# Ten half-tiles take their threshold on GpSimd: one exponential in place of an exponential and a masked pass

## The chip, the cores and the metric

One NeuronCore of a Trainium2 chip runs the whole program. It has five engines that run their own instruction streams in order: TensorE (PE in the profile, with its weight loads apart as PEld), VectorE (DVE), ScalarE (ACT), GpSimd (POOL) and SyncE (SP), which here issues most of the DMA transfers. The metric is the device time of one execution in microseconds (us); lower is better.

## The reference

Sixty-four heads (8 batches of 8 heads, 576 positions, head width 64) of attention with a threshold, and then a three-way maxout feed-forward layer over 4608 tokens:

```
scores = scale * q @ k.T                       # scale = 1/8
thresh = max(scores, axis=-1) - tau            # tau = 0.02
scores = where(scores >= thresh, scores, -1e9)
attn   = exp(scores - max(scores)); attn /= sum(attn) + 1e-9
x      = attn @ v                              # heads side by side: 4608 x 512
h      = max(x @ w1, x @ w2, x @ w3)           # 512 -> 768
out    = h @ w_out                             # 768 -> 512
```

Every row of scores keeps only the entries within tau of its maximum; all others count as zero.

## The kernel before, in words

**Tiles.** The heads are taken four at a time (a quad, two per batch). A quad has 9 chunks of 128 partitions by two halves of 576 keys; the unit of work is such a half-tile, 128 x 576, and there are 288 of them, called tiles below. For each tile the program does: `S`, the scores in fp32 on TensorE into one of four PSUM slots (`sc`); `m`, the row maximum on VectorE (`nm` receives it); then one of two ways to the numerators, chosen tile by tile by a digit of the table `MASKED`:

- digit 0: ScalarE takes a Prelu of the scores that multiplies the positive side (the excluded entries) by one and the kept side by 2^-100 (`e`, tile `z<-sc,nm`), and then an exponential with scale -2^100, which brings the kept side back and sends the excluded side to zero, with the row sum as a second result (`n`). Two passes on ScalarE, and one on VectorE, the maximum.
- digit 1: the maximum pass also writes the negated scores to SBUF (`z<-sc`); ScalarE takes the exponential (`e`, `z<-z,nm`); VectorE then keeps what is at least exp(-tau) and sums it (`k`, a SCALAR_TENSOR_TENSOR). One pass on ScalarE and two on VectorE.

**After the numerators.** For the first batch (the first 36 tiles, quads 0 and 1) the numerators go straight into the bf16 tile `P`, unnormalised; the sums are gathered in `sums`, inverted for a whole part (`R`), spread over a PSUM tile by small matmuls (`D`, tile `d`), copied to `wide` (`b`), and multiplied in when the attention product is copied to `xt` (`w`). For all other batches the numerators go to fp32 `z`, and GpSimd scales them into `P` (`p`, `P<-z,rs`). Then SyncE issues a DMA transpose of `P` (`t`, `ptq<-P`), TensorE multiplies by v (`O` and `N`, tile `o`), the result becomes `xt`, and TensorE runs the feed-forward matmuls (`F` and `B`, tiles `ph` and `po`). There are six `P` buffers, each for a pair of tiles, and a new one waits until the transpose of the one six before it has read it. There are eight `z` tiles.

**Other work of GpSimd.** It copies halves of the transposed queries to the other partitions (`q`, `qs<-qt`; scores need them), and casts v (`y`) and the weights (`z` in the table) to bf16.

**What sets the order.** `ORDER` is a string written out by hand or by a planner; each letter issues one step, so it fixes the order of the instructions on every engine and of the DMAs in SyncE's queue. `_Ordered` chains the instructions of each engine in that order, and an instruction that waits holds up all behind it on its engine. Nearly all instructions go through that helper, so the profile names them by line 92 and by their tiles.

Of the kernel before, what the change touches and what calls it, by code (L numbers as in the profile page):

```python
# [40 lines left out]
ORDER = """
mS2S3lmS1meenemelllgkllT0S2aqmlmeS3lmgT1lllT0eqckT2ancS0mtqS1qmennktyS3eteS2mznmS1eeS0mnlS3eS2S1mmS3netmegke
S2mS0mmyeS3znnRytyltleeS1nmkkeS0mmeeS2mS1enS0T3kmmktgltlemS1D2aS0eT3blekmmteS2D0O1ckmlO3bNwRwS0mneeD1knS3beT
2nD1tllabS0mS2ketnO1lRktmetmO3qNqtwqwzenT2nS0S1zncS3qymmS2mmeeS1S3D0S2mkmtD1elbeemneS0kmbkT3S1kegmatS2qS3neT
0memknneS2O1O3cNtS0remkwtqerT2pnaRmpS1D0gekrS2bmtlwneS0S3D1mmpplleblppzO2eO1mrqpNnekpS0wwS2nnmzF3S1S0emrmrmk
glBepqpF1pF2ethgzBevT3nBF0S1nncBvhS3S2pmrmgF0ekeT1BatnmrF3vS1BS0peF2rmpypS1lpBnvmezF3nhzBS2mpenekqvS1F0F3mtm
BqerkrBpgvepptT2cS1T0hnamttS3mnrS2tF0myBeS1ppeS2yvnplF3rS0nmemteeBlF1meqptS2pvT3BcmnF0tlS3znkphgglBemS1rvmS2
O3npemO0rknrNeewpF1xpS2qpS0ltntmF3lmneeBBS2S0rvhmF1tntpzleS3mBpF0S2empztvenrpBmpvS1mnS3S2enF0emrpS3pktS1pnme
rmmepBekuS2mkunenrS1S3pF0T2pmmtaBeueukpS1rpqeklmeS2tO3mprO0ekNS1lltlwlS2xmF3nF0BmepT1kBehrcF2nT3T1BvcppS0tlq
aqnllvF3qlmS1mrBprF2S0nekheBnmpvtF3S1BF2eS0mvtprmBypnpS1ehpytpS3mtoS2oeelmtmS0F3lF1meBkevryBT2yenF0vapT3cBT2  # L50
S1lS3naqhpF2qS0rkmBpmmrF3npeS1vempteneBvF2S0ktpmltrllBF3S1lnhnmBqrvpneelS0S2mpmO1ekreO3NT0xS2wcmS3mnpqpnF1F0
pBekpBvS2ertlS3F1htmtltmS0pBnemepynrF3eS2vS0mmrT1atppqeBS2pnpF1vF3meultkS0klT1enormkT2BaS2peS0ortcmnmuurS1pe
T2qpF3cS2mpenenpS0kmetrBmltS1S2puymlueeqpS0pylomO3mO1knNerekxwS0pmS2F3S1npnqmBF2elS0kmtBerkheF3pS1nmeypvBtrm
noF2leS0vpBS3rrmnpmpphS1ppF0etmS2emllBeF1nF3BtevkrpS0BvS2nS1hmmtleS3lmmetF2tkF0eBpleT1BvrvanT3nF2cS1BnmF0S3B
rhkF2mpeT1vnrBpprveaS0S3nmT1S2pqpncmpS0meeeqmeS1tO3pqmtotlloeO2ltqNF0S1klwBxrpkppS3mrhmF2S0epBmF3nenS1pvBF0m
F2nleBBtottvkS3hF0keF1rurvpmT2BeapkppyrpvS1S3mnS2S0pnemF1mtS2emkS3rpBenepltS0memkmrutpuS3neS2emF1rmpqkynpS3p
qeBemS0uuS3O2kmemekO1NeS0rwT3xoF1olppnT2mnT0BcS3aS2rncqhF0qtF1pBtemmpBkevrF3eS2vlmpnBptnlS0S1S2hermmempS3F0y
pmF1BBelrteoevnF2T3F0akkqvBBS3nhkymF1pqpnF2verBBS0rvtpmhnS3S1F2mrmlpBpeS0evlmS3eF1pnS2BmnleF3mtllvrlttS0eppp
tyBmS1ehF2lepT3BmltnS0lnltcS1rkvO3O2tmNpmeprT1nnexrapkwS0pqF2qyemT1T3cpBF0S1anepkBS3hvF2S0mreBF1mekmrnvF3qBe
S2vS0unpS3tS1omlrmeppqptlmmnF2pktT0BpecS1eekryuT3uaS0mnS2lomtmrtleF3enpS1kpS2qppnemmS0BmkerppeueqS1S0mnurO2k  # L60
mO1NkwxT0S3eeS1cmpmF2F0kkeBBhF3eF2pvrBS1nnBvpttS0hmemS3mrppF1rpS2BeenmeF0S3vBF1nkvmS2mlnBS0otolhF3llterlmF1k
BlpypvpBtvteeprS2F0rT3BpS1nnrmpmaS3mtpheS0S2emnF3eT1T0amecBS2ttoS0evyymmS1ppeO3mpqneO2NenqxF0kktF1wBT3lolrlk
lBpS2vphS0cmnF1mtlteS3nqrtBmrpF0vrpqpF2lekBeBpnhF1S3vmT0tlpBS2lS3avmpF0tF1mBrnelekS2evutppmrS3qppS1nS0nmF2mr
mS1peekenpS3BemmeS0rkS1emuS3tlT0ueT2mcknrannpepF1S0mS2qppBmtotlmlttkrrpeueS0qqmS2lO3ueemoeO0opptpkklNwS1lS2x
F3mS0BnemehF1kT2mrcnpBS0F3rvS2BltlpnmF1nepmeveS0pkmBS3httnF2eF1mBrBekF0nS3vrBprvpypppS2nmhemeS1S0F2pF3mmBeBr
T1eS0kvnapS2vF1nS3mnBrmmreS2F0pheS1meeBqpnS3mvmeypS1tpS2etlO0qO3mNpmT2neytF1xtlkkrtnweS3ppT0cramBF2S0Bnehvpp
meS1rF3qqmT2BF0ncveT2ktnBF3vS1mrnarBhppS0lF2T3qppeBmcS0S1ovmF3mneT2naepBvS0S2enF3mkmrkqpqueenF1nS3tmS0T2cpqB
eupurrS2mmottoS3pS0mttneelotpmS1O2mkkO0rNwrpeexpneF3nkpS0S2S1mBemS0euuppmF1erkS2tltlBptmrF3S0lhtpmeyppBeS1mv
O0O2NenmxpS3S1kF0mxemrS2kBF1enF3vBermF0tBhpyppyektBvS1pmF2F3vBkS1BF0nmehS2vrBmtpO3eotpnevO1NkF0S2krmnrpxpxBh
F3S1eBF0mS2F1BnvpmBrS3vS2S0ehemmF1kppmnF3rBvkBF2F0BF1ehBtkvevoF2pptkttO3O0NuprBwS2xS0vmmpeS3ekF1S2pmF0oeBmrB  # L70
okettF3peuokoruoF2uhF1pkkF3hvvruF2pF1F3hppF0pvvF2F1vvF3F0F2hvtovhtF1F3F0F2htvF1voF3O0uvO2NvF1xwF3hF2F0vF3vhF
2F0F3hvF2vvF0F3F2vF0hF3hovF2vF0F3vhF2vvF0vBuuF3BuouoF2uooo
"""


# [731 lines left out]
```

## Time and profile before

| | |
|---|---|
| median of 3 runs | 441.56 us (440.37 to 443.75) |
| the profiled execution | 439.98 us, of which 438.2 us from first to last instruction (the span) |
| busy: PE, DVE, ACT, POOL | 96%, 91%, 88%, 66% of the span |
| mean granted TensorE clock | 1.00 |

A row of the profile's groups reads: line, engine, operation, output tile <- input tiles, shapes, count | busy time, mean ns of one | idle time of the engine just before these instructions and what ended it. On DVE and ACT the recorded durations of neighbours overlap a little; what an instruction costs its engine is read from start to start in the timeline.

### The profile page before, as it was taken

Reading aid. Unit: us, or ns where it says so; the run is one execution under the profiler, and the core shown is the slowest. Engines: PE = TensorE matmul, PEld = TensorE weight load, DVE = VectorE, ACT = ScalarE, POOL = GpSimd, SP = SyncE. Lnnn points to the kernel's source line nnn. Section 1 sums busy time; section 2 is a strip of 40 time slices with the busy share of each in tenths; the row PEclk is TensorE's granted clock in tenths of the full one; section 3 lists DMA queues with packets and bytes.
Section 4 is the critical chain, followed back from the end, with each engine's and each line's share of the span. In section 5 each row is a group of like instructions: output and inputs, shape, how many; then the busy total and the mean of one; then the engine's idle time right before and its main releaser. Section 6 shows DMA issues by size and latency. Waiting matters only on the chain.

```text
span 438.2 us, 14262 instructions
## 1 busy us (share of the span) xinstructions
PE 420.6 (96%) x5313; PEld 306.9 (70%) x5313; DVE 398.2 (91%) x1105; ACT 387.0 (88%) x784; POOL 288.5 (66%) x370
## 2 busy tenths in 40 slices
PE   7679889999999999999999999999999999999995
PEld 5446458776787767867787767877677776777762
DVE  3999999989999999999999999999999999999641
ACT  5999999999999999988999999989999999875422
POOL 3704288978688697596867885678759677554500
PEclk9999999999999999999999999999999999999999
DMA  7999999999999999999899998979989997485602
GB/s 252 302 241 206 221 229 261 237 244 193 211 192 225 229 200 193 205 174 256 185 203 216 222 190 206 212 201 219 201 220 186 246 150 154 110 160 128 177 14 109
DMA packets 212773, 87.45 MB, mean 200 GB/s; under 512 B 185824, under 2 KB 199648, under 8 KB 212704
## 3 DMA queue, kind: packets, MB, share of 16 engines
q1 hardware_dynamic: 212000, 85.69, 92.4%
q8 instruction: 42, 0.69, 0.7%
q10 hardware_dynamic: 704, 0.85, 0.6%
q14 instruction: 27, 0.22, 0.2%
HBM read 34.60 MB, written 9.44 MB: 101 GB/s over the span
## 4 chain that ended last, share of the span: by engine, by line
PE 81%; ACT 9%; DMA 3%; issue 2%; DVE 2%; POOL 2%; SPq 0%; POOLq 0%; DVEq 0%
PE ph L92 30%; PE sc L92 27%; PE po L92 11%; PE o L92 9%; ACT z L92 5%; PE tp L92 3%; DMA ptq<-P 3%; ACT P L92 2%; POOL P L92 1%; DVE z L92 1%; PE warm L92 1%; DVE unused L92 1%; ACT qt L92 1%; DMA out_dram<-ob 1%; PE d L92 0%
## 5 line engine op out<-in xcount | busy, mean ns | idle before, releaser
L92 POOL TENSOR_SCALAR P<-z,rs 128x576 bf16<-128x576 f32 x252 | 206.8, 833 | 78.9 <-DVE rs L92 27.4
L92 PE MATMUL sc<-kt,qt 64*128 64x256 f32 (+2 forms) x640 | 177.1, 421 | 2.7 <-DVE z L92 1.3
L92 PE MATMUL sc<-kt,qs 64*128 64x320 f32 (+2 forms) x640 | 175.5, 410 | 4.0 <-ACT z L92 1.6
L92 PE MATMUL ph<-xt,w 64*128 64x288 bf16 (+4 forms) x2160 | 170.5, 283 | 0.4 <-ACT z L92 0.2
L92 PEld LDWEIGHTS <-w 64*128 64x128 bf16 (+1 forms) x2160 | 124.4, 94 | 33.6 <-issue 6.3
L92 DVE TENSOR_SCALAR_CACHE_REDUCE unused<-sc 128x576 bf16<-128x576 f32 x170 | 124.8, 749 | 4.0 <-PE sc L92 3.2
L92 ACT ACTIVATE z<-sc,nm 128x576 f32<-128x576 f32 x170 | 122.7, 740 | 3.4 <-DVE unused L92 1.6
L92 PEld LDWEIGHTS sc<-kt,qs 64*128 64x128 f32 (+1 forms) x640 | 91.0, 175 | 19.7 <-ACT z L92 6.3
L92 ACT ACTIVATE z<-z 128x576 f32<-128x576 f32 x151 | 102.3, 682 | 0.2
L92 PEld LDWEIGHTS sc<-kt,qt 64*128 64x128 f32 (+1 forms) x640 | 90.4, 175 | 16.3 <-DVE z L92 4.3
L92 ACT ACTIVATE z<-z,nm 128x576 f32<-128x576 f32 x118 | 89.5, 773 | 4.8 <-DVE z L92 4.6
L92 DVE TENSOR_SCALAR_CACHE_REDUCE z<-sc 128x576 f32<-128x576 f32 x118 | 87.5, 751 | 5.6 <-PE sc L92 3.1
L92 DVE SCALAR_TENSOR_TENSOR z<-z 128x576 f32<-128x576 f32 x101 | 80.1, 802 | 0.1
L92 POOL COPY qs<-qt 64x640 f32<-64x640 f32 (+3 forms) x68 | 47.8, 702 | 42.3 <-ACT qt L92 27.7
L92 PE MATMUL po<-wo,hT 64*128 64x512 bf16 (+1 forms) x480 | 53.6, 357 | 0.1
L92 ACT ACTIVATE hm<-ph 128x576 bf16<-128x576 f32 (+4 forms) x54 | 32.1, 594 | 19.9 <-PE ph L92 19.5
L92 DVE TENSOR_TENSOR hm<-ph,hm 128x576 bf16<-128x576 f32 (+4 forms) x54 | 36.9, 684 | 8.5 <-PE ph L92 8.4
L92 PEld LDWEIGHTS <-hT 64*128 64x128 bf16 (+1 forms) x480 | 26.3, 97 | 20.0 <-issue 3.9
L92 DVE TENSOR_TENSOR hT<-ph,hm 128x576 bf16<-128x576 f32 (+4 forms) x54 | 37.1, 688 | 2.4 <-PE ph L92 0.5
L92 PE MATMUL o<-ptq,vb 128*64 128x64 bf16 (+2 forms) x576 | 36.5, 275 | 0.8 <-DMA ptq<-P 0.8
L92 PEld LDWEIGHTS <-vb 128*64 128x64 bf16 x576 | 23.3, 111 | 15.7 <-issue 5.1
L92 ACT ACTIVATION_READ_ACCUMULATOR z<-z 128x1 f32 x151 | 30.0, 199 | 0.0
(40 smaller groups left out, 297.3 us busy)
## 6 DMA issues: line engine op xcount, KB each, us to landing
vm<-in_v_dram SPq DMA_DIRECT2D x32, 256.0 KB, 4.7
out_dram<-ob SPq DMA_DIRECT2D x31, 256.0 KB, 3.2
qm<-in_q_dram SPq DMA_DIRECT2D x15, 512.0 KB, 4.8
km<-in_k_dram SPq DMA_DIRECT2D x15, 512.0 KB, 5.5
stage<-in_moe_w_dram SPq DMA_DIRECT2D x9, 512.0 KB, 5.8
ptq<-P SPq DMA_TRANSPOSE x144, 4.2
stage<-in_moe_w_out_dram SPq DMA_DIRECT2D x3, 512.0 KB, 5.5
qm<-in_q_dram SPq DMA_DIRECT2D x16, 64.0 KB, 3.2
```

The lines of the kernel that those rows point to most:

```text
L92: ins = fn(*a, **kw)
```

## The change

A third kind of tile, digit 2, is added. Its maximum pass is that of digit 1 (it writes the negated scores `z`). Then GpSimd does three instructions (`d`): it adds tau to the negated maximum (`limit`, one column), compares `z` with `limit` and writes 2^100 where the entry is excluded and 0 where not into the tile's own half of `P`, and adds that to `z` in place. ScalarE then takes one exponential from `z` into `P` with the row sum (`j`): the excluded entries come out as zero. So a tile of digit 2 costs one pass on VectorE, one on ScalarE and three instructions on GpSimd.

Ten of the first 36 tiles in the table get digit 2 (tiles 5, 8, 11, 14, 17, 20, 23, 26, 29, 32). Within those 36, seven fewer have digit 1 and three fewer digit 0. Nine digits further on (up to tile 120) change between 0 and 1. In all there are now 166 of digit 0, 112 of digit 1 and 10 of digit 2, where there were 170 and 118. `ORDER` is new over its first 1086 steps (130 of 288 scores); what follows is the same, but for PSUM slots 2 and 3, which have changed names.

```
-001011001000011010101101101000010111100001101000010100001010000100001000
+001002002002102012012102112002012110100001101000010100001010000001001010
...
+    def excluded(c, r):
+        zn, far, limit = c["z", r], half_of(c, r), small.tile([128, 1], F32, name="limit", bufs=2)
+        pool.tensor_scalar(out=limit, in0=c["bias", r], scalar1=tau, scalar2=None, op0=OP.add)
+        pool.tensor_scalar(out=far, in0=zn, scalar1=limit, scalar2=1.0 / FLAT, op0=OP.is_gt, op1=OP.mult)
+        pool.tensor_tensor(out=zn, in0=zn, in1=far, op=OP.add)
+
+    def kept(c, r):
+        scalar.activation(out=half_of(c, r), in_=c["z", r], func=AF.Exp, bias=c["bias", r], scale=-1.0,
+                          accum_out=sum_of(c, r))
...
 -        if masked(c["g"], c["idx"], r):
+        if kind_of(c["g"], c["idx"], r) != "0":
...
+        elif what == "d":
+            c, r = line["d"].pop(0)
+            excluded(c, r)
+            line["j"].append((c, r))
+        elif what == "j":
+            c, r = line["j"].pop(0)
+            kept(c, r)
```

**GpSimd, second quad (the swaps of its queries, and the first casts).** Before, the stretch holds only swaps (`qs<-qt`) and casts:

```order
L92 COPY qs_262<-qt_261 64x2x320 [waits Activation_49]
L92 COPY qs_262<-qt_261 64x2x256 [waits Activation_49]
L92 CAST vb_348<-vm_129 128x1024 [waits DMAHW7_49,DMAHW6_49,Pool_49]
L92 CAST w0_63<-stage_239 128x4x256 [waits DMAHW6_49]
L92 CAST vrb_432<-vr_130 128x128 [waits DMAHW1_49,DMAHW0_49]
```

The same stretch now (`limit`, then `P<-z,limit`, then `z<-z,P` are the three instructions of one tile):

```order
L92 COPY qs_255<-qt_254 64x2x320 [waits Activation_49]
L92 TENSOR_SCALAR limit_327<-nm_297 128x1 [waits DVE_49,Pool_49]
L92 TENSOR_SCALAR P_309<-z_298,limit_327 128x576 [waits Pool_49]
L92 TENSOR_TENSOR z_298<-z_298,P_309 128x576 [waits Pool_49]
L92 COPY qs_255<-qt_254 64x2x256 [waits Activation_49,Pool_49]
L92 CAST vb_353<-vm_129 128x1024 [waits DMAHW7_49,DMAHW6_49,Pool_49]
L92 CAST w0_63<-stage_320 128x4x256 [waits DMAHW3_49]
L92 TENSOR_SCALAR limit_387<-nm_338 128x1 [waits DVE_49]
L92 TENSOR_SCALAR P_386<-z_339,limit_387 128x576 [waits Pool_49]
L92 TENSOR_TENSOR z_339<-z_339,P_386 128x576 [waits Pool_49]
```

The first three-instruction group stands between the two pairs of swaps, and each of its instructions waits for the one before it.

**GpSimd, third quad.** Here the groups stand around the swaps of the next quad's queries; some of the `P<-z,limit` also wait for a DMA (`DMAHW`), the transpose that frees the `P` buffer:

```order
L92 CAST w2_65<-stage_448 128x4x256 [waits DMAHW4_49]
L92 CAST vb_579<-vm_227 128x1024
L92 COPY qs_572<-qt_571 64x2x320 [waits PE_49,Activation_49,Pool_49]
L92 CAST vrb_647<-vr_228 128x128 [waits DMAHW0_49,Pool_49]
L92 TENSOR_SCALAR limit_651<-nm_604 128x1 [waits DVE_49]
L92 TENSOR_SCALAR P_650<-z_605,limit_651 128x576 [waits DMAHW3_49,Pool_49]
L92 TENSOR_TENSOR z_605<-z_605,P_650 128x576 [waits Activation_49,Pool_49]
L92 COPY qs_572<-qt_571 64x2x320 [waits Pool_49]
L92 TENSOR_SCALAR limit_717<-nm_687 128x1 [waits DVE_49,Pool_49]
L92 TENSOR_SCALAR P_716<-z_688,limit_717 128x576 [waits DMAHW6_49,Pool_49]
L92 TENSOR_TENSOR z_688<-z_688,P_716 128x576 [waits Pool_49]
L92 COPY qs_572<-qt_571 64x2x256 [waits Activation_49,Pool_49]
```

Before, no group stood there: the four swaps of that quad followed each other with two casts between them.

**ScalarE, tiles 8 to 14 and around.** Before, all that ScalarE waits for here comes from VectorE, from itself or from a DMA:

```order
L92 ACTIVATE z_387<-sc_368,nm_378 128x576 [waits DVE_49]
L92 ACTIVATE P_404,sums1_71<-z_373 128x576 [waits Activation_49]
L92 ACTIVATE z_406<-sc_375,nm_395 128x576 [waits DVE_49]
L92 ACTIVATE z_399<-z_399,nm_398 128x576 [waits DVE_49]
L92 ACTIVATE z_410<-z_410,nm_409 128x576 [waits DVE_49]
L92 ACTIVATE z_434<-sc_392,nm_420 128x576 [waits DVE_49]
L92 ACTIVATE P_404,sums1_71<-z_387 128x576 [waits Activation_49]
L92 ACTIVATE P_441,sums1_71<-z_406 128x576 [waits DMAHW7_49,Activation_49]
```

Now three exponentials of the new kind (`P<-z,nm`) stand in the same stretch, and each waits for GpSimd:

```order
L92 ACTIVATE P_386,sums1_71<-z_339,nm_338 128x576 [waits Pool_49]
L92 ACTIVATE z_378<-z_378,nm_377 128x576 [waits DVE_49]
L92 ACTIVATE P_401,sums1_71<-z_395 128x576 [waits Activation_49]
L92 ACTIVATE z_423<-sc_380,nm_415 128x576 [waits DVE_49]
L92 ACTIVATE z_434<-sc_408,nm_428 128x576 [waits DVE_49]
L92 ACTIVATE z_432<-z_432,nm_431 128x576 [waits DVE_49]
L92 ACTIVATE P_401,sums1_71<-z_375,nm_374 128x576 [waits Pool_49]
L92 ACTIVATE wide0_104<-d_441 128x256 [waits PE_49]
L92 ACTIVATE P_436,sums1_71<-z_419,nm_418 128x576 [waits DMAHW6_49,Pool_49]
```

ScalarE's stream has one instruction for such a tile where it had one or two, and a wait for a third engine.

More of the change, by code (lines that the diff above doesn't have):

```diff
@@ L47 @@
[L47 to L56, printed above, removed]
@@ new lines @@
+S3etznBmhT2F0BF1mrckvegprS2peBF3nmS0pBnvS1ephmF2ekmrT3BapvS0egS3F2tS1mtnF0BmrmzeBpzpnF1lehnenyBS3vkvmrS2F0eF
+1tBmBS3keqhrgtT2pT1vS0ppntaqppcS2znmmeemF1rBvenS3mnF0S2eS1rmBttF2meppevnT3BphctS0tnS1meF3mkgeS2Bqtnnpqrlvrml
+eppS1mtrkO0O3NgF1xlS2pnwS3llF0pBBmmeepkvS2ezF3mrhneS1ylmS0mprlBvnF2tS1pemBppzyS3penenvS0rmS1pF2mS0enpmekkemt
+S3rtnButS1mtrppS0F3lupkmerekT2tamkBpeS2lpquS0uS1tlO3lmenmmkO2eeetNlxS0rS1wmlF3mpneF2BT0kpypehrcnBF1T3aptlT0q
+nBlpnvcS2vF3qmS0ermrqBF1S2hekBmF3pnepvlnypS0BF1mS2vrBmyppeS3S0phememS2S1F0moeF3eBmBkT2eF1vT0rnaBnT2hpvckS3ma
@@ new lines @@
+S0F1pqneS2tqnmrprtBmF0S3vBemrF1veppS2BnS0tehF3ktplmS1lmrytlpoBmnnS2vO0relqmeO3pNeetT1S2pqppkwplotxclmS3lmnF0
+nkF1BeBS2evS3rmhmpttnlrF0S1tBS3mvpmeenerpF2S1pT0BpmlvpS3yaneF0uomeklkF2rS0T1enkT3tmacrBneS3uS1mS0tT3mupqtemt
+clF2epS1tepS3rypllltnpnpnS0kmBemtreS3mS0lqlO1pummpuO2NS0eeekS3xknrnpwmF2S1pmBqkletF3ehS0mrokqemnpBpvF2S1BrF3
+epyonmS0verrBS2mnpmpphS1ppF0etmS3emllBeF1nF2BtevkrpS0BvS3nS1hmmtleS2lmmetF3tkF0eBpleT1BvrvanT2nF3cS1BnmF0S2B
+rhkF3mpeT1vnrBpprveaS0S2nmT1S3pqpncmpS0meeeqmeS1tO2pqmtotlloeO3ltqNF0S1klwBxrpkppS2mrhmF3S0epBmF2nenS1pvBF0m
@@ new lines @@
+F3nleBBtottvkS2hF0keF1rurvpmT3BeapkppyrpvS1S2mnS3S0pnemF1mtS3emkS2rpBenepltS0memkmrutpuS2neS3emF1rmpqkynpS2p
+qeBemS0uuS2O3kmemekO1NeS0rwT2xoF1olppnT3mnT0BcS2aS3rncqhF0qtF1pBtemmpBkevrF2eS3vlmpnBptnlS0S1S3hermmempS2F0y
+pmF1BBelrteoevnF3T2F0akkqvBBS2nhkymF1pqpnF3verBBS0rvtpmhnS2S1F3mrmlpBpeS0evlmS2eF1pnS3BmnleF2mtllvrlttS0eppp
+tyBmS1ehF3lepT2BmltnS0lnltcS1rkvO2O3tmNpmeprT1nnexrapkwS0pqF3qyemT1T2cpBF0S1anepkBS2hvF3S0mreBF1mekmrnvF2qBe
+S3vS0unpS2tS1omlrmeppqptlmmnF3pktT0BpecS1eekryuT2uaS0mnS3lomtmrtleF2enpS1kpS3qppnemmS0BmkerppeueqS1S0mnurO3k
@@ L73 @@
+okettF2peuokoruoF3uhF1pkkF2hvvruF3pF1F2hppF0pvvF3F1vvF2F0F3hvtovhtF1F2F0F3htvF1voF2O0uvO3NvF1xwF2hF3F0vF2vhF
+3F0F2hvF3vvF0F2F3vF0hF2hovF3vF0F2vhF3vvF0vBuuF2BuouoF3uooo
 """
@@ L311, in masked, with kind_of @@
     def masked(g, idx, r):
-        return by_mask[2 * number[g, idx] + r] == "1"
+        return kind_of(g, idx, r) == "1"
+    def kind_of(g, idx, r):
+        return by_mask[2 * number[g, idx] + r]
     def z_of(c, r):
@@ L337, in exponents, with half_of, sum_of @@
             scalar.activation(out=zn, in_=c[r], func=AF.Prelu, bias=c["bias", r], scale=-1.0, alpha=FLAT)
+    def half_of(c, r):
+        if "P" not in c:
+            c["P"] = pp.tile([128, W], BF16, name="P")
+        return c["P"][:, r * S:(r + 1) * S]
+    def sum_of(c, r):
+        at = 2 * PLACE[c["idx"]] + r
+        return sums[c["g"]][:, at:at + 1]
+    def excluded(c, r):
[6 more added lines that the diff above has]
+                          accum_out=sum_of(c, r))
     def numerators(c, r):
@@ L342, in numerators @@
         if g < 2:
-            if "P" not in c:
-                c["P"] = pp.tile([128, W], BF16, name="P")
-            to, acc = c["P"][:, r * S:(r + 1) * S], sums[g][:, 2 * PLACE[idx] + r:2 * PLACE[idx] + r + 1]
+            to, acc = half_of(c, r), sum_of(c, r)
         else:
@@ L631 @@
                 O=products(), F=pieces())
-    line = {k: [] for k in "menkrptahvuxwcqNb"}
+    line = {k: [] for k in "menkrptahvuxwcqNbdj"}
     line["R"] = [(g, part) for part in range(2) for g in range(2)]
@@ L677, in issue @@
             c["bias", r] = maximum(c, r)
-            line["e"].append((c, r))
+            line["d" if kind_of(c["g"], c["idx"], r) == "2" else "e"].append((c, r))
+        elif what == "d":
[5 more added lines that the diff above has]
+            kept(c, r)
+            c["halves"] = c.get("halves", 0) + 1
         elif what == "e":
```

38 lines of the change are left out of this document (15 added, 23 removed).

## The prediction

> **What bounds the kernel now.** I read the page first, then busy time by stage, then the chain of waits, and last the timelines of the engines that the chain names.
>
> ```profile
> span 438.2 us, 14262 instructions
> PE 420.6 (96%) x5313; PEld 306.9 (70%) x5313; DVE 398.2 (91%) x1105; ACT 387.0 (88%) x784; POOL 288.5 (66%) x370
> POOL 3704288978688697596867885678759677554500
> ```
>
> TensorE is busy for 96% of the span, but these are averages: GpSimd's row of 40 slices starts with a hole (the digits 0, 4 and 2 in slices of 11 us), and that is where the new work goes. The stages show what bounds each (columns: length, then busy time of PE, PEld, DVE, ACT and POOL with counts, clock, DMA share, GB/s):
>
> ```profile
> 0.00:10.00 10.00, 7.92 (x71) 6.14 (x73) 2.88 (x7) 4.54 (x10) 3.21 (x12) 1.00 0.77 239
> 10.00:36.00 26.00, 19.54 (x193) 12.26 (x189) 25.86 (x75) 25.72 (x53) 10.65 (x15) 1.00 1.08 261
> 36.00:52.00 16.00, 13.97 (x155) 8.82 (x154) 15.51 (x46) 15.57 (x35) 4.76 (x5) 1.00 1.13 236
> 52.00:66.00 14.00, 11.99 (x171) 7.43 (x171) 12.97 (x39) 13.59 (x30) 11.06 (x13) 1.00 1.07 215
> 66.00:80.00 14.00, 13.91 (x200) 11.29 (x197) 13.63 (x40) 13.46 (x28) 12.70 (x16) 1.00 1.09 248
> 80.00:200.00 120.00, 119.66 (x1562) 89.39 (x1560) 115.45 (x322) 116.70 (x237) 93.48 (x120) 1.00 1.06 211
> 200.00:400.00 200.00, 199.92 (x2661) 148.41 (x2658) 192.44 (x537) 183.71 (x370) 145.46 (x186) 1.00 0.93 194
> ```
>
> From 10 to 52 us VectorE and ScalarE are both full (41.4 and 41.3 of 42 us), TensorE has holes (8.5 us), and the DMA engines are full as well. From 66 us on TensorE is full: 334 us with half a us idle. So anything gained on VectorE or ScalarE after 66 us is hidden by TensorE, and a gain must come from TensorE starting its saturated stretch earlier, or with more of its work done. It starts with the first feed-forward matmul (`ph`), and this is what stands ahead of it:
>
> ```profile
> 63.20 1.31 PE L92 MATMUL o<-ptq,vb 128*64 128x256 bf16 x31 [0.77 <-DMA ptq<-P]
> ...
> 65.89 0.60 PE L92 MATMUL ph<-xt,w 64*128 64x256 bf16 x7
> ```
>
> The chain of waits between 10 and 66 us says the same, by line and in its longest pieces:
>
> ```profile
> by line: ACT z L92 29.8%; DMA ptq<-P 21.6%; ACT P L92 17.8%; issue 10.5%; DVE z L92 4.5%; ACT qt L92 2.9%; PE o L92 2.9%; PE sc L92 2.5%; PE d L92 2.4%; DVE unused L92 1.7%; ACT wide L92 1.7%; DVE P L92 1.1%; DVE xt L92 0.8%; PE tp L92 0.6%
> 43.98 6.91 DMA ptq<-P
> 57.98 5.17 DMA ptq<-P
> ```
>
> Half of it is ScalarE (z, P, qt, wide: 52%), a fifth the transposes of `P`, and VectorE comes to 8%. The engine that the change relieves most is the one the chain names least.
>
> **The change part by part: VectorE and ScalarE.** Costs go from start to start:
>
> ```profile
> 17.05 0.73 ACT L92 ACTIVATE z<-sc,nm 128x576 f32<-128x576 f32 x1
> 17.68 0.77 ACT L92 ACTIVATE z<-z,nm 128x576 f32<-128x576 f32 x1
> 18.34 0.68 ACT L92 ACTIVATE P<-z 128x576 bf16<-128x576 f32 x1
> 18.91 0.20 ACT L92 ACTIVATION_READ_ACCUMULATOR P<-z 128x1 f32 x1
> 19.01 1.36 ACT L92 ACTIVATE z<-sc,nm 128x576 f32<-128x576 f32 x2
> ...
> L92 ACT ACTIVATE qt<-tp 128x640 f32<-128x640 f32 x3 | 2.1, 707 | 0.0
> L92 ACT ACTIVATE wide<-d 128x256 f32<-128x256 f32 x4 | 1.5, 382 | 0.3 <-PE d L92 0.3
> ...
> 22.16 0.75 DVE L92 SCALAR_TENSOR_TENSOR P<-z 128x576 bf16<-128x576 f32 x1
> 22.83 0.08 DVE L92 DVE_READ_ACCUMULATOR P<-z 128x1 f32 x1
> ```
>
> A Prelu costs ScalarE 0.63 us, the exponential of digit 1 0.66, that of digit 0 0.67 with 0.10 of it for the sum. The new one has the column `nm` and the sum, so 0.66 + 0.10 = 0.76. VectorE's masked pass costs 0.67; its maximum pass stays for every tile.
>
> Up to the point in the order where all first 36 tiles have their numerators, I count 40 maxima in both kernels, and on VectorE 17 masked passes before against 10 now: 7 x 0.67 = 4.7 us less. On ScalarE 20 Prelus, 18 and 19 exponentials before; 18, 11, 16 and ten new ones now: -2 x 0.63 - 7 x 0.66 - 3 x 0.67 + 10 x 0.76 = -0.3 us. With four query copies at 0.6 and six of `wide` at 0.29 (their rows less the 0.1 by which neighbours overlap), ScalarE has 41.1 us of work from its first Prelu at 8.58 us to that point: it can't be there before 49.7. Before, VectorE was the later of the two:
>
> ```profile
> 51.67 0.76 DVE L92 SCALAR_TENSOR_TENSOR P<-z 128x576 bf16<-128x576 f32 x1
> ```
>
> It ends at 52.4. So of VectorE's 4.7 us at most 2.7 count, before any wait for GpSimd. Over the whole program VectorE has 6 masked passes less (4.0 us) and ScalarE 4 x 1.30 + 6 x 0.66 - 10 x 0.76 = 1.6 us less; past 66 us both are hidden by TensorE.
>
> **GpSimd.** No instruction of before reads two tensors on it. These rows are nearest:
>
> ```profile
> L92 POOL TENSOR_SCALAR P<-z,rs x252: 737/745/1838, 56.1 to 410.3; 128x576 bf16<-128x576 f32 x126
> L92 POOL TENSOR_SCALAR P<-z,rs 128x576 bf16<-128x576 f32 x252 | 206.8, 833 | 78.9 <-DVE rs L92 27.4 <-issue 24.5 <-ACT z L92 14.5
> L788 POOL MEMSET const-float32-0.0<- 128x1 f32 x1 | 0.1, 98 | 0.2 <-issue 0.2
> L92 POOL CAST w<-stage 128x1024 bf16<-128x1024 f32 x6 | 6.7, 1122 | 0.1
> L92 POOL COPY qs<-qt 64x640 f32<-64x640 f32 x6 | 4.4, 735 | 20.3 <-PE d L92 11.4 <-ACT qt L92 8.8
> L92 POOL COPY qs<-qt 64x512 f32<-64x512 f32 x5 | 4.1, 826 | 6.5 <-ACT qt L92 6.4
> L92 POOL CAST vb<-vm 128x1024 bf16<-128x1024 f32 x3 | 3.1, 1036 | 0.1
> L92 POOL CAST vrb<-vr 128x128 bf16<-128x128 f32 x2 | 0.6, 288 | 0.0
> 12.66 1.48 POOL L92 COPY qs<-qt 64x640 f32<-64x640 f32 x2 [1.67 <-ACT qt L92]
> ```
>
> The one-column `limit` is 0.1 us. The compare has one tensor and one column in and bf16 out, as the scaling of `P` has: 0.745 undisturbed. The add lies between one such pass (0.745) and two (1.49); it reads two tensors, so I take 1.4. The two hand-overs between the dependent three are no row of their own; 0 to 0.1 each, and I take 0.1 for both. That is 2.35 us undisturbed, bounds 1.6 and 2.5. The scaling row's mean is 12% above its median, which is what neighbours cost here; with half of that I take 2.5 us a tile, and as the far end 4.5, where both long passes are held as long as the worst row (1.838, so 1.1 more each).
>
> The Trainium skill, GPSIMD Engine Reference, section Performance versus the Vector engine, says that two inputs share one read port and gives about 2.6 cycles an element at 1.2 GHz. An estimate from that page is 576 x 2.6 / 1.2 = 1.25 us for the add; no trace here shows it, and by it each tile would be 0.15 cheaper and the waits of 2.1 us worked out next would shrink to 0.8.
>
> Does ScalarE wait? Its queue holds everything behind a `P<-z,nm` that waits, and TensorE's PSUM slots with it. GpSimd starts on the second quad's swaps when their queries are copied, at 12.66 before; one Prelu less stands ahead of that copy now, so 12.0. Up to the seventh group it has 7 x 2.5, two swaps of 0.735 and two of 0.826, one `vb` 1.04, two weight casts of 1.12 and one `vrb` 0.29: 24.2 us, done at 36.2. ScalarE's own work up to its seventh new exponential (12 Prelus, 7 and 11 exponentials, 6 new ones, 3 copies, 2 of `wide`) ends at 35.1: 1.1 us late. To the ninth group there are two more groups, a weight cast, a `vb`, a `vrb` and two swaps, 8.9 us, done at 45.1, where ScalarE would come at 43.0: 2.1 late in all. The tenth has time to spare. So the 36 tiles end at 49.7 + 2.1 = 51.8 instead of 52.4.
>
> **Behind the tiles.** That 0.6 us has to pass SyncE's queue, whose transposes are late anyway:
>
> ```profile
> 54.09 6.19 SPq L92 DMA_TRANSPOSE ptq<-P  x3
> ```
>
> The three transposes of this row stand in the same place of the queue in both orders, behind the same DMAs, and are issued from 54.09 on although their last numerators were there at 52.4. So I let nothing of the 0.6 through. On TensorE the new order has one score tile more ahead of the first `ph` (50 from the table against 49). Its price:
>
> ```profile
> 200.00:300.00 100.00, 42.99 (x308) 25.70 (x308) 49.59 (x137) 30.15 (x42) 1.00 1.00 211
> ```
>
> This row is the score tile `sc` alone: 42.99 us for 308 of 1280 matmuls, that is 69 of 288 tiles, 0.62 us each. It moves into TensorE's holes, and the saturated stretch is shorter by as much. The later flips between 0 and 1 lie under a full TensorE and I cost them at nothing; if their cover failed they would move one masked pass more, 0.67 us.
>
> **The sum.** 0 from the tiles and -0.6 from TensorE: 439.98 - 0.6 = 439.4 against the profiled execution. That one lies 1.6 below the median of the runs, so against the median 441.0. A change of under 1% (4.4 us) is about what a measurement of this kernel can't tell from none; its three runs alone span 3.4 us.
>
> **The rivals.**
>
> *GpSimd becomes the bound (slower).* Every 0.1 us on a group moves the ninth by 0.9. The transposes leave 1.7 us (52.4 to 54.09) and the tiles' end 0.6 on top, so from 2.75 us a group on, each further 0.1 costs 0.9 at the end. At 3.5 us, halfway up to the far end, it is 0.9 x 7.5 = 6.7 later, less 0.6: 441.6 + 6.1 = 447.7. For it: GpSimd would be busy without a pause from 12 to 36 us, and the 1.838 row. Against it: the median is 0.745.
>
> *VectorE's gain comes through whole (faster).* If ScalarE's pieces in the chain only follow VectorE, the first stage ends 4.7 earlier: 441.6 - 4.7 - 0.6 = 436.3. Against it: ScalarE's 41.3 of 42 us busy, and the transposes.
>
> *VectorE is held by GpSimd.* Masked passes show it:
>
> ```profile
> L92 DVE SCALAR_TENSOR_TENSOR z<-z x101: 730/754/1331, 54.4 to 406.8; 128x576 f32<-128x576 f32 x101
> ```
>
> The worst is 0.6 us longer than the shortest. Ten such passes are left in the stage; all held so long give 6.0 us, against 4.7 saved and the 1.7 us of the transposes: no more than 441 to 442. The Trainium skill, SBUF — State Buffer, section Who interferes with whom, has this as a lock: a VectorE instruction with two SBUF inputs and a GpSimd instruction that reads SBUF hold each other up. By that rule the spread in this row is the lock, and the trace agrees so far.
>
> *A `P` buffer is late.* The compare claims `P` some us before ScalarE needs it, and some compares wait for a transpose; GpSimd's swaps and casts queue behind.
>
> ```profile
> DVE P L92 <- DMA ptq<-P: 0.4, 2, 0.2
> ```
>
> Before, VectorE waited so twice, 0.2 us each. If four compares wait 1 us each, the ninth group is 6.1 late in place of 2.1: 1.7 later at the end, 442.7.
>
> **How the numbers follow.** Forecast 441.0: 0.48. GpSimd the bound: 0.24, of which 0.18 lies over 1% slower (from 3.3 us a group). VectorE's gain whole: 0.10, of which 0.07 is over 1% faster. The lock 0.08 and the late buffer 0.10, of which 0.02 over 1% slower. So faster 0.07, same 0.73, slower 0.20. The range takes in half of the gain rival and GpSimd's case up to just under 3.5 us a group: 437 to 447.5.
>
> **What would show it.** Right: the three GpSimd instructions sum to 2.3 to 2.6 us; ScalarE waits for GpSimd 1 to 3 us in all before 50 us; VectorE gets holes of some 4 us there; the first `ph` starts within 1 us of 65.9; the 36 tiles end near 52. Wrong: waits of ScalarE for GpSimd over 5 us (the bound moved), a first `ph` before 63 (the transposes weren't late of themselves), or TensorE with new holes between 66 and 200 us, which would mean that the new order costs something that I put at nothing.

## The result, and the profile after

The changed kernel takes 454.50 us (median of four runs, 453.88 to 455.34), the kernel before 442.65 on the same chip (440.37 to 443.82): a ratio of 1.0266, interval 1.0219 to 1.0313. The forecast was 441.0, range 437 to 447.5. It is slower by 11.9 us between medians. Between the two profiled executions (454.66 and 439.98) it is 14.7; the one of before lies low among its own runs, and the medians are the better measure. One run of `f1_fill` below fell in a slower state of the chip and is left out.

The page of the changed kernel, busy time and two rows of the 40 slices:

```profile
PE 430.0 (95%) x5313; PEld 312.9 (69%) x5313; DVE 397.1 (88%) x1093; ACT 386.1 (85%) x786; POOL 326.8 (72%) x400
POOL 3899988998876968857787797576877767653500
PEclk9986689999999999999999999999999999999999
```

GpSimd's hole at the start is filled to 8 and 9 tenths. TensorE's granted clock was full before; it now dips within that stretch, most from 34 to 57 us (the two digits 6). The stages of the changed kernel, in the prediction's windows (length, busy PE, PEld, DVE, ACT, POOL, clock, DMA share, GB/s):

```profile
10.00:36.00 26.00, 16.10 (x131) 9.59 (x128) 17.04 (x47) 18.30 (x40) 23.14 (x25) 0.92 1.04 244
36.00:52.00 16.00, 12.90 (x102) 8.00 (x104) 11.79 (x30) 10.24 (x23) 15.16 (x13) 0.71 0.82 185
52.00:66.00 14.00, 12.69 (x104) 7.74 (x106) 9.52 (x27) 11.12 (x23) 13.05 (x13) 0.74 0.80 159
66.00:80.00 14.00, 12.65 (x182) 7.92 (x176) 13.41 (x41) 13.98 (x32) 11.90 (x14) 1.00 0.77 167
80.00:200.00 120.00, 119.67 (x1573) 90.72 (x1573) 116.50 (x323) 117.70 (x240) 96.83 (x122) 1.00 1.02 217
```

VectorE and ScalarE, full before from 10 to 52 us, are now two thirds busy (28.8 and 28.5 of 42 us). From 80 us on everything is as before. The first `ph`, from the timeline of TensorE:

```profile
81.11 0.60 PE L92 MATMUL ph<-xt,w 64*128 64x256 bf16 x8
```

It stood at 65.89 and stands 15.2 us later; the execution is 14.7 longer. So the whole loss is made before the first `ph`. The chain of waits doesn't reach back into that stage in this trace; three of the longest waits (8 to 75 us; total, times, longest) and GpSimd's timeline do:

```profile
ACT P L92 <- POOL z L92: 10.8, 6, 3.3
DVE z L92 <- ACT P L92: 5.4, 3, 3.7
DVE z L92 <- PE sc L92: 5.4, 5, 2.2
```

```profile
14.57 0.24 POOL L92 TENSOR_SCALAR limit<-nm 128x1 f32<-128x1 f32 x1
14.91 2.23 POOL L92 TENSOR_SCALAR P<-z,limit 128x576 bf16<-128x576 f32 x1
17.21 1.27 POOL L92 TENSOR_TENSOR z<-z,P 128x576 f32<-128x576 f32 x1
18.55 1.25 POOL L92 COPY qs<-qt 64x512 f32<-64x512 f32 x2
...
30.21 0.70 POOL L92 TENSOR_SCALAR limit<-nm 128x1 f32<-128x1 f32 x1
...
56.55 0.23 POOL L92 TENSOR_SCALAR limit<-nm 128x1 f32<-128x1 f32 x1
56.87 2.22 POOL L92 TENSOR_SCALAR P<-z,limit 128x576 bf16<-128x576 f32 x1
59.17 1.27 POOL L92 TENSOR_TENSOR z<-z,P 128x576 f32<-128x576 f32 x1
...
63.28 2.22 POOL L92 TENSOR_SCALAR P<-z,limit 128x576 bf16<-128x576 f32 x1
65.59 1.54 POOL L92 TENSOR_TENSOR z<-z,P 128x576 f32<-128x576 f32 x1
```

Look at the compare, `P<-z,limit`: 2.2 us in each group, where the prediction had 0.745. The three instructions between 10 and 70 us (count | busy, mean ns of one | idle before):

```profile
L92 POOL TENSOR_SCALAR P<-z,limit 128x576 bf16<-128x576 f32 x10 | 22.2, 2223 | 0.9
L92 POOL TENSOR_TENSOR z<-z,P 128x576 f32<-128x576 f32 x10 | 13.1, 1309 | 0.8
L92 POOL TENSOR_SCALAR limit<-nm 128x1 f32<-128x1 f32 x10 | 3.2, 318 | 0.9
```

Ten groups, each from the start of `limit` to the end of the add, take 3.89 to 4.37 us, 4.02 in the mean, and GpSimd is busy for 50.8 of the 54.1 us from 13.0 to 67.1, the gaps being little more than hand-overs.

### The profile page after: what moved, and what is told of

The parts are those of the page before. It is cut to its first block, busy times and chain, and to the rows that moved or that the text cites. A ratio compares the mean times of both kernels' runs of the same rounds, so it can differ in the third digit from the quotient of the medians.

```text
span 452.9 us, 14303 instructions
## 1 busy us (share of the span) xinstructions
PE 430.0 (95%) x5313; PEld 312.9 (69%) x5313; DVE 397.1 (88%) x1093; ACT 386.1 (85%) x786; POOL 326.8 (72%) x400
## 4 chain that ended last, share of the span: by engine, by line
PE 82%; ACT 3%; DVE 1%; DMA 1%; issue 0%; SPq 0%; DVEq 0%; ACTq 0%
PE ph L92 32%; PE sc L92 28%; PE po L92 10%; PE o L92 8%; PE tp L92 3%; ACT z L92 2%; DMA out_dram<-ob 1%; ACT P L92 0%; DVE unused L92 0%; ACT wide L92 0%; ACT qt L92 0%; DVE obr L92 0%; DVE xt L92 0%; DVE z L92 0%; SPq L92 0%
## 5 line engine op out<-in xcount | busy, mean ns | idle before, releaser
L92 PE MATMUL sc<-kt,qt 64*128 64x256 f32 (+2 forms) x640 | 185.1, 436 | 4.9 <-ACT wide L92 3.0
L92 PE MATMUL sc<-kt,qs 64*128 64x320 f32 (+2 forms) x640 | 183.7, 425 | 4.9 <-POOL qs L92 3.1
L92 PEld LDWEIGHTS <-w 64*128 64x128 bf16 (+1 forms) x2160 | 125.7, 94 | 33.2 <-issue 6.2
L92 DVE TENSOR_SCALAR_CACHE_REDUCE unused<-sc 128x576 bf16<-128x576 f32 x166 | 122.2, 748 | 8.7 <-PE sc L92 7.6
L92 ACT ACTIVATE z<-sc,nm 128x576 f32<-128x576 f32 x166 | 119.7, 738 | 3.9 <-DVE unused L92 1.5
L92 PEld LDWEIGHTS sc<-kt,qs 64*128 64x128 f32 (+1 forms) x640 | 93.5, 181 | 22.1 <-POOL qs L92 4.9
L92 PEld LDWEIGHTS sc<-kt,qt 64*128 64x128 f32 (+1 forms) x640 | 92.9, 181 | 20.0 <-ACT wide L92 4.6
L92 DVE TENSOR_SCALAR_CACHE_REDUCE z<-sc 128x576 f32<-128x576 f32 x122 | 90.8, 752 | 16.1 <-PE sc L92 8.5
L92 ACT ACTIVATE z<-z,nm 128x576 f32<-128x576 f32 x112 | 85.0, 771 | 4.5 <-DVE z L92 4.4
```

What stands on the lines that cost most here:

```text
L92: ins = fn(*a, **kw)
```

## The experiments

All medians stand beside the kernel before on the same chip (442.9 to 443.4); the ratios with their intervals are those on record, and not the quotients of these medians. "Group" is the mean of the ten spans from the start of `limit` to the end of the add in the profiled execution. Three theories were to be told apart: that the **length** of GpSimd's group sets the time, through its own queue and ScalarE's waits; that the **compare** does it by holding VectorE at SBUF; and that the **clock** of TensorE, or the **new order**, does it of itself.

### A quick pass in place of the compare

In `e2_mult` the compare becomes two multiplications of the same shapes; nothing is cut off by the threshold in those ten tiles.

```diff
-        pool.tensor_scalar(out=far, in0=zn, scalar1=limit, scalar2=1.0 / FLAT, op0=OP.is_gt, op1=OP.mult)
+        pool.tensor_scalar(out=far, in0=zn, scalar1=limit, scalar2=1.0, op0=OP.mult, op1=OP.mult)
```

> The changed kernel, its order and all its waits, with the compare replaced by two multiplications (the threshold is left out of the ten tiles, so their numerators are others). A group on GpSimd should take 0.25 + 0.75 + 1.27 + 0.25 = 2.5 us in place of 4.0. Theory 'GpSimd's time per group is the whole loss': the time returns to 441 (438 to 444), first feed-forward matmul within 2 us of 65.9, no stretch at half clock after the first one. Rival 'the new order itself is bad': the time stays at 449 or more.

442.57 us, ratio 0.9986 (0.9960 to 1.0012): the whole loss is gone, with the new table, the new order and all hand-overs in place. The group is 2.70 us in the mean. What lies behind the last group is the same in both kernels; the windows from the end of the last group to the first `ph`, first of the changed kernel, then of this one:

```profile
67.13:81.11 13.98, 12.63 (x176) 8.25 (x177) 13.39 (x42) 13.96 (x32) 11.72 (x15) 1.00 0.75 157
```

```profile
53.51:67.50 13.99, 12.78 (x177) 8.25 (x176) 13.39 (x42) 13.99 (x32) 11.71 (x16) 1.00 1.06 215
```

13.98 and 13.99 us. Ten groups are 1.32 us shorter each, 13.2 us, and the last ends 13.6 us earlier. So the new order does no harm of itself.

In both windows ScalarE is busy throughout (13.96 and 13.99 us, 32 instructions). So what lies between GpSimd's last group and the first `ph` is ScalarE's queue, and the end of that group sets the first `ph` as long as the same work is left in that queue. In `p2_price` and `g1_first5`, described below, more is left, 39 and 35 instructions; the window is longer, and ScalarE is again busy throughout:

```profile
57.55:74.44 16.89, 14.91 (x212) 9.96 (x212) 16.19 (x50) 16.89 (x39) 11.70 (x15) 1.00 0.80 184
```

```profile
59.91:75.25 15.34, 13.64 (x187) 8.68 (x185) 14.75 (x46) 15.26 (x35) 11.72 (x15) 1.00 0.85 192
```

### The same length without a compare

`e3_mult_1` issues that line of two multiplications twice, `e4_mult_2` three times.

```diff
+        pool.tensor_scalar(out=far, in0=zn, scalar1=limit, scalar2=1.0, op0=OP.mult, op1=OP.mult)
```

> As the one with two multiplications, but that instruction twice (a group of about 3.3 us). Theory 'GpSimd's time': beyond about 2.75 us a group every 0.1 us costs 0.9 us, so 446 (444 to 449). Rival 'it is the compare itself, by holding VectorE's masked passes': 441 to 443, since no compare is left.

> As the one with two multiplications, but that instruction three times (a group of about 4.1 us, as long as the changed kernel's, without any compare). Theory 'GpSimd's time': 453 to 455, with the half-clock stretches of the changed kernel. Rival 'the compare itself': 441 to 446.

450.81 us (1.0157, 1.0115 to 1.0198) and 459.03 us (1.0341, 1.0292 to 1.0391). GpSimd's timeline of `e4_mult_2`; shown are the passes of its first group, and the passes and the add of its last:

```profile
14.96 2.43 POOL L92 TENSOR_SCALAR P<-z,limit 128x576 bf16<-128x576 f32 x3
...
65.99 3.32 POOL L92 TENSOR_SCALAR P<-z,limit 128x576 bf16<-128x576 f32 x3
69.39 1.79 POOL L92 TENSOR_TENSOR z<-z,P 128x576 f32<-128x576 f32 x1
```

`e4_mult_2` has no comparison in its groups and is slower than the changed kernel: the time follows the group's length, whatever fills it, and the compare is nothing special but long. It came out above the 453 to 455 expected; the three passes together took 2.42 to 3.39 us, and so its group is 4.48 us long and not 4.1. From 2.70 to 4.48 us of group the median rises by 16.5 us, 0.92 for each 0.1 us.

### Half of the groups short

`g1_first5` keeps the compare in the first five groups and takes the two multiplications in the last five; `g2_last5` is the reverse.

```diff
+        nth.append(0)
+        if len(nth) <= 5:
             pool.tensor_scalar(out=far, in0=zn, scalar1=limit, scalar2=1.0 / FLAT, op0=OP.is_gt, op1=OP.mult)
+        else:
+            pool.tensor_scalar(out=far, in0=zn, scalar1=limit, scalar2=1.0, op0=OP.mult, op1=OP.mult)
```

> The changed kernel with the compare in the first five of the ten tiles and two multiplications in the last five (the threshold is left out there). Theory 'GpSimd has no pause, so every group counts alike': half of the loss between two multiplications everywhere (442.6) and the compare everywhere (454.5), so 448 to 449. Rival 'only the groups late in the stage count, since the early ones have slack before the transposes': under 445.

> The changed kernel with two multiplications in the first five of the ten tiles and the compare in the last five. Theory 'every group counts alike': 448 to 449, as with the first five. Rival 'only the late groups count': 452 or more.

449.63 us (1.0192, 1.0141 to 1.0242) and 448.94 us (1.0165, 1.0119 to 1.0212). By the medians each half alone costs about half of the loss (6.7 and 6.0 of 11.9 us); by the ratios it is more, 1.9 and 1.7 of 2.7 per cent, each half a per cent either way. Both halves cost, and neither the whole: no single place in the order catches the loss, and both rivals (under 445 for the first five, 452 or more for the last five) are refuted.

### No GpSimd work at all

`e5_nogroup` leaves out the three instructions of the group (and with them the threshold in ten tiles). VectorE keeps its relief, and ScalarE waits for GpSimd nowhere.

```diff
-        zn, far, limit = c["z", r], half_of(c, r), small.tile([128, 1], F32, name="limit", bufs=2)
-        pool.tensor_scalar(out=limit, in0=c["bias", r], scalar1=tau, scalar2=None, op0=OP.add)
-        pool.tensor_scalar(out=far, in0=zn, scalar1=limit, scalar2=1.0 / FLAT, op0=OP.is_gt, op1=OP.mult)
-        pool.tensor_tensor(out=zn, in0=zn, in1=far, op=OP.add)
+        half_of(c, r)
```

> The changed kernel with GpSimd's three instructions left out of the ten tiles (their excluded entries are not removed); the order and all else stay. It bounds what taking ten thresholds off the two other engines can bring at best. Theory 'ScalarE and the transposes hold the first stage anyway': 440 to 442.5, no different from the kernel before by more than 0.5%. Rival 'VectorE's 4.7 us would come through if GpSimd were quick enough': 436 to 438, with the first feed-forward matmul near 61.

442.32 us, 1.0002 (0.9968 to 1.0036). Even free, the change wins nothing. The chain of waits of this run from 10 to 69 us, by line:

```profile
by line: DMA ptq<-P 18.6%; ACT P L92 17.4%; ACT z L92 17.2%; PE sc L92 13.0%; issue 7.7%; DMA qm<-in_q_dram 6.8%; PE o L92 6.0%; DVE unused L92 4.1%; PE d L92 3.5%; DVE kt L92 2.3%; ACT wide L92 2.1%; ACT qt L92 2.0%; DVE z L92 1.6%; DVE P 
```

ScalarE (P, z, wide and qt: 38.7%) and the transposes of `P` (18.6%) lead here too, and VectorE's shown lines come to 8.0%, as before. So what was taken from VectorE was not what the stage waited for.

### The old order with the new kind of tile

Three kernels take the table and `ORDER` of before and turn some tiles of digit 1 into digit 2 at their old places (`e` becomes `d`, `k` becomes `j`): tiles 5, 8, 14, 20, 23 and 26 with GpSimd's work left out (`b1_old_free`) and with it (`b2_old_six`), and 14, 20 and 26 with it (`b3_old_three`). The first row of the table in the first two:

```diff
-001011001000011010101101101000010111100001101000010100001010000100001000
+001012002000012010102102102000010111100001101000010100001010000100001000
```

> The order of the kernel before, with six of its first 36 tiles (5, 8, 14, 20, 23, 26, all of digit 1 there) turned to the new kind in place: their exponential moves to where the masked pass stood, and GpSimd's three instructions are left out (their excluded entries are not removed). VectorE loses 6 x 0.67 = 4.0 us, ScalarE gains 0.6, nothing else moves. Theory 'the first stage is held by ScalarE and the transposes, so relief of VectorE is worth nothing in any order': 441 to 443. Rival 'the new order hid the relief': 438 to 439.5.

> The same six tiles in the old order, with GpSimd's three instructions (about 4.0 us a tile, 24 us in all) standing where their exponential stood. GpSimd's holes between 21 and 52 us were some 24 us. Theory 'it is GpSimd's time in the first stage': the groups fill the holes and run over by some us, 444 to 449. Rival 'the loss came from the new order': 441 to 443.

> As the one with six, for tiles 14, 20 and 26 alone, with their threshold on GpSimd. 12 us of GpSimd's work in holes of some 24 us. Theory 'GpSimd's time counts only once the holes are full, and relief of VectorE is worth nothing': 441 to 444. Rival 'even a few groups in its in-order queue hold up the swaps and casts behind them': 445 or more.

443.44 us (0.9990, 0.9960 to 1.0019), 445.58 us (1.0047, 1.0020 to 1.0074) and 442.93 us (1.0007, 0.9972 to 1.0042). In the old order too the relief alone is worth nothing: six masked passes less on VectorE, no gain. Six groups of 3.90 us there cost half a per cent, three cost nothing that shows. So the loss is not bound to the new order: it is a matter of how much time of GpSimd is asked for in a stretch, and three groups fit into its hole. No version that was run beats the kernel before, and `e5_nogroup` and `b1_old_free` say that in these two orders a cheaper group wouldn't either.

### The clock

`f1_fill` is the changed kernel with three transposes of an identity on TensorE behind each of the first 54 score tiles, into a part of the slot that nobody reads.

```diff
+        filled.append(0)
+        if len(filled) <= 54:
+            for _ in range(3):
+                tensor.transpose(ps[:, 832:960], identf, identf)
```

> The changed kernel with three idle transposes of the identity on TensorE after each of the first 54 score tiles, into columns that nobody reads, so that TensorE is busier while it waits. Theory 'GpSimd is the bound and the half clock is only a follow-up': the granted clock stays at 1.0 or nearly so in the first 80 us and the time changes by less than 2 us (453 to 456). Rival 'the half clock takes a good part of the loss': with the clock back the time falls to 450 or less. If the clock stays down all the same, the run tells nothing of it.

463.03 to 468.36 us in three runs, ratio 1.0592 (1.0512 to 1.0672). In the profiled execution the clock is back (mean 0.999), the group is as long as in the changed kernel (4.08 us), and the last one ends at 69.14, not earlier than the 67.13 of the changed kernel. But the fill is 27.9 us of TensorE work on the way of the scores: from 8 to 75 us VectorE now waits 14.5 us for them (8.2 and 6.3) against 10.0, and the tail behind the last group grows from 14.0 to 19.5 us. So neither forecast came, and this run doesn't give the price of the half clock.

That price is bounded by the changed kernel itself. Behind GpSimd's last group the clock is full (1.00 in the window above). Ahead of it GpSimd is idle for 3.3 us in all from 13.0 to 67.1, so a faster TensorE could not have ended that group more than 3.3 us earlier, of a loss of 11.9. What part of the 3.3 us the clock has, no run shows.

### What a pass of GpSimd costs, by operation

`e1_price` and `p2_price` put ten different passes in the place of the ten compares, in the order of the tiles: they read and write the same tiles, and only the operation differs.

```diff
-        pool.tensor_scalar(out=far, in0=zn, scalar1=limit, scalar2=1.0 / FLAT, op0=OP.is_gt, op1=OP.mult)
+        form = forms.pop(0)
+        ops = {1: (OP.add, 1.0, OP.mult), 2: (OP.mult, 1.0, OP.add), 3: (OP.mult, None, None), 4: (OP.add, None, None),
+               5: (OP.subtract, None, None), 6: (OP.is_gt, None, None), 7: (OP.add, 1.0, OP.add)}
...
+                pool.tensor_scalar(out=far, in0=zn, scalar1=limit, scalar2=second, op0=op0, op1=op1)
+        elif form == 8:
+            pool.tensor_copy(out=far, in_=zn)
+        elif form == 9:
+            pool.tensor_tensor(out=far, in0=zn, in1=limit.to_broadcast([128, S]), op=OP.subtract)
+        elif form == 10:
+            pool.tensor_tensor(out=far, in0=zn, in1=zn, op=OP.mult)
```

These are the lines of `p2_price`. Those of `e1_price` have the same build, with mult·mult, subtract·mult, is_gt alone, is_gt·mult against a constant, is_ge·mult, is_gt·mult to fp32 in place, subtract·max, max alone, subtract·min and is_gt·mult.

> The changed kernel's ten compares are replaced, tile by tile in the order of the program, by ten forms: two multiplications; subtract and multiply; is_gt alone; is_gt and multiply with a constant for the limit; is_ge and multiply; is_gt and multiply with fp32 output in place; subtract and max; max alone; subtract and min; and the original is_gt and multiply. The result is another in nine of the ten tiles. Theory 'the comparison is what is dear on GpSimd': the forms with is_gt or is_ge take 2.0 to 2.3 us, the arithmetic ones 0.74 to 0.8; max and min tell whether selecting is dear as well (open: 0.75 or 1.3 or more). Rival 'it is the bf16 output or the pointer to the limit that is dear': two multiplications also take over 2 us, and the fp32 or the constant form is short. Span: about 445 if most forms are short, 452 if none is.

> The changed kernel with the compare replaced, tile by tile, by ten other forms (the thresholds are left out): add and multiply; multiply and add; multiply alone; add alone; subtract alone; is_gt alone; add and add; a copy with a cast to bf16; a two-tensor subtract with the limit broadcast; a two-tensor multiply. The first price list had 0.75 us for two multiplications, 1.74 for is_gt or max alone and 2.23 for every other pair. Theory 'only multiplying has a quick form': multiply alone 0.75, the copy 0.66, all other single ones 1.74 and pairs 2.23. Rival 'adding is as quick as multiplying, and only subtracting, comparing and selecting are slow': add alone and the two mixed pairs 0.75. The two-tensor forms: 1.27 for both by either.

GpSimd's timeline in `e1_price`: mult·mult, subtract·mult, is_gt alone, is_gt·mult with a constant, and max alone:

```profile
14.57 0.75 POOL L92 TENSOR_SCALAR P<-z,limit 128x576 bf16<-128x576 f32 x1
...
20.47 2.23 POOL L92 TENSOR_SCALAR P<-z,limit 128x576 bf16<-128x576 f32 x1
...
24.71 1.74 POOL L92 TENSOR_SCALAR P<-z,limit 128x576 bf16<-128x576 f32 x1
...
28.20 2.16 POOL L92 TENSOR_SCALAR P<-z 128x576 bf16<-128x576 f32 x1
...
48.46 1.74 POOL L92 TENSOR_SCALAR P<-z,limit 128x576 bf16<-128x576 f32 x1
```

The other five pairs (is_ge·mult, is_gt·mult to fp32, subtract·max, subtract·min, is_gt·mult) took 2.23 each. The same view of `p2_price`: add·mult, mult·add, mult alone, add·add, the cast, and the product of two tensors:

```profile
14.72 0.74 POOL L92 TENSOR_SCALAR P<-z,limit 128x576 bf16<-128x576 f32 x1
...
20.63 0.75 POOL L92 TENSOR_SCALAR P<-z,limit 128x576 bf16<-128x576 f32 x1
...
23.36 1.74 POOL L92 TENSOR_SCALAR P<-z,limit 128x576 bf16<-128x576 f32 x1
...
39.13 2.24 POOL L92 TENSOR_SCALAR P<-z,limit 128x576 bf16<-128x576 f32 x1
...
46.56 0.66 POOL L92 CAST P<-z 128x576 bf16<-128x576 f32 x1
...
55.05 1.15 POOL L92 TENSOR_TENSOR P<-z 128x576 bf16<-128x576 f32 x1
```

Add, subtract and is_gt alone took 1.74 to 1.75, the two-tensor subtraction of the spread limit 1.15. Most forms were run once; mult·mult and is_gt·mult stand in all ten groups of `e2_mult` and of the changed kernel. So it is not the comparison alone that is slow, nor is it multiplication that is quick: mult alone takes 1.74. That refutes both theories of `p2_price`, only multiplying is quick and adding is as quick. Of all that was measured, three pairs are quick (mult·mult, add·mult, mult·add), the other pairs cost 2.2 us and a single operation 1.7. The row that priced the compare, the scaling of `P`, is two multiplications in the kernel (by `rs` and by 1.0), and so one of the quick ones. Why these are quick no run shows. As whole kernels the two, run once each, gave 451.26 and 450.64 us, with groups of 3.72 and 3.15 us.

## Why the prediction was wrong

**What bounds the kernel: right.** The time of a profiled execution less the start of its first `ph` is 374.1 us before and 373.6 after; it lies between 373.4 and 375.5 in all other runs but `p2_price` (376.2), while the first `ph` itself goes from 65.9 to 88.7. All of the change happens ahead of it, and the flips of digits later on cost nothing that shows.

**VectorE's relief hidden by ScalarE and the transposes: right**, in both orders (`e5_nogroup`, `b1_old_free`). The rival that it comes through whole is refuted. That the relief is worth nothing is measured; that ScalarE and the transposes are what hides it rests on the chains of waits, and no run tells the two apart.

**The price of the group: the step that failed.** "The compare has one tensor and one column in and bf16 out, as the scaling of `P` has: 0.745 undisturbed." It takes 2.22. The row was chosen by shape and types, and the operation decides. The other terms of the group were near: the add 1.27 against 1.4, the hand-overs 0.07 to 0.10 each against 0.1 for both, `limit` 0.23 against 0.1 (0.66 and 0.70 in two of the three that follow straight on another group). For the add the Trainium skill, GPSIMD Engine Reference, section Performance versus the Vector engine, gave an estimate of 1.25 us; the trace agrees, 1.27 where nothing disturbs it. The bounds "1.6 and 2.5" did not hold the 4.02 that came; only the far end of 4.5 did, for another reason than it was given (both passes held up).

**What followed from it: right, once the price is put in.** The ninth group was to be done at 45.1 and ended at 60.44. Start to start, the first nine groups take 36.4 us in place of 22.5: 13.9 later; the first swaps start at 13.0 in place of 12.0: 1.0; the casts and copies between make the last 0.4. The rival *GpSimd becomes the bound* had a rule, 0.9 us for each 0.1 us of group above 2.75, less 0.6. With the measured groups, on the median of before on the same chip:

| kernel | group, us | by the rule | measured | ScalarE waits for GpSimd, us |
|---|---|---|---|---|
| e2_mult | 2.70 | 442.8 | 442.6 | 1.5 |
| p2_price (one run) | 3.15 | 446.3 | 450.6 | 5.7 |
| g1_first5 | 3.32 | 447.4 | 449.6 | 7.4 |
| g2_last5 | 3.33 | 447.5 | 448.9 | 6.7 |
| e3_mult_1 | 3.51 | 449.6 | 450.8 | 7.9 |
| e1_price (one run) | 3.72 | 451.5 | 451.3 | 7.9 |
| the change | 4.02 | 453.5 | 454.5 | 10.8 |
| e4_mult_2 | 4.48 | 458.4 | 459.0 | 14.4 |

The rule is low by 1 to 2 us in the timed kernels of the middle and 4.3 low for `p2_price`; for the change itself it is 1.0 short. Of the 4.3, 2.9 are the longer ScalarE queue behind the last group (16.89 against 13.98 us), which the rule doesn't have, and it explains the longer window of `g1_first5` too. The last column (8 to 75 us of the profiled execution) follows the loss almost one for one: 10.8 us of waits for 11.9 us lost, 14.4 for 15.6, 1.5 for none. So the mechanism stood among the rivals with about the right price per step. It was given 0.24 and a price at 3.5 us a group, because "the median is 0.745" was counted against it. A median of another operation was no evidence.

**The lock on VectorE: there, and small.** The masked passes of the stage (10 to 70 us), before and then after:

```profile
L92 DVE SCALAR_TENSOR_TENSOR P<-z 128x576 bf16<-128x576 f32 x17 | 12.8, 760 | 0.4 <-DMA ptq<-P 0.4
```

```profile
L92 DVE SCALAR_TENSOR_TENSOR P<-z 128x576 bf16<-128x576 f32 x10 | 9.3, 934 | 1.1 <-ACT z L92 1.1
```

0.17 us more on each of ten, 1.7 us on an engine with holes of 13 us. The compare as the cause of the loss by that lock is refuted by `e4_mult_2`, which has the loss without a compare, and by `e2_mult`, where the same passes take 1.02 us in the mean and nothing is lost. **A late `P` buffer**: in the changed kernel GpSimd waits for no transpose; it did not come to it. **TensorE's -0.6**: run less first `ph` is 0.5 smaller after than before, as it should be, but the other kernels scatter by more, so it is not settled.

**The signs that were named.** ScalarE's waits for GpSimd are 10.8 us, over the 5 that were to mean a moved bound, and that is what happened. TensorE does have new holes from 66 to 80 us (12.65 busy of 14, before 13.91), since the first `ph` has moved past them to 81; from 80 to 200 us it has none (119.67 of 120). By this sign alone the new order would have been blamed, which `e2_mult` refutes.

## What to carry to other kernels

Price an instruction by a row of the same operation, with the same number of operations in it; a row of equal shape and types is no price, and where there is none, the range has to span what that engine's other operations cost before an engine with a hole is called free. Where work is moved to an engine with a hole, add up that engine's whole queue over the stage in order: up to the edge (here about 2.7 us a group) it costs nothing, and past it every tenth of a us counts about as often as there are groups. Relieving an engine wins nothing while another one beside it is as full; leaving the new work out altogether shows that in one run.
